# A state-space convolution mixed with an MLP by a gate: the taps' factors, powers and products laid out with each channel's samples side by side

## The chip, the cores and the metric

The kernel runs on one core of one Trainium2 chip. The metric is the device time of one execution in microseconds (us), the median of several runs. The engines are named as in the profile: PE is TensorE (PEld its weight loads), DVE is VectorE, ACT is ScalarE, POOL is GpSimd, SP the queue of SyncE, which issues most of the DMAs.

## What is computed

There are L = 2048 positions, D = 512 channels and NS = 128 states per channel. Branch a is a convolution along the positions, with taps made from the states; branch b is an MLP with 1792 hidden columns; a gate g per position mixes the two.

```python
g = sigmoid((x * gate_w).sum(-1, keepdims=True))
# a: taps K of each channel, then a causal convolution and a skip
P = exp((dt * (A_re + 1j * A_im))[:, :, None] * l)      # l = 0 .. 2047
K = einsum("dn,dnl,dn->dl", C, P, dt * B).real
y = irfft(rfft(pad(K)) * rfft(pad(u)))[:L] + u * Dskip
# b
h = gelu(x @ w1 + b1)
return g * y + (1 - g) * (h @ w2 + b2)
```

The change lies in the making of K.

## The kernel before

**Two parts.** `front` holds the MLP, the first stage of the transforms of the signal and of the taps, and the making of the taps. `conv` loads the transformed signal and taps back from HBM, multiplies them, transforms back and mixes. In the profile `front` fills some 0 to 402 us and `conv` the rest.

**How `front` is ordered.** Every piece of work in `front` is a task of a planner (`Plan`): an engine, a fixed cost, what it reads and writes, and a due time from the list `DUES`. `pl.run()` plays the tasks through once, on the host and with the fixed costs, and issues them in that order. On the chip each engine then works off its own instructions strictly in that order; an instruction whose input is late holds up all those behind it on its engine. The MLP (`hidden`, L985 to L1012; `output`, L1028 to L1060), the signal's first stage (`first_stage`, L489) and the taps are interleaved in this way. The MLP's matmuls are split into high and low halves: ScalarE makes the gelu (L1002) and the high half `hh` (L1005), VectorE the low half `hl` (L1012), TensorE multiplies both.

**The taps.** A tap of channel d at position l = 64 p + q is a sum over the 128 states of a factor for p times a factor for q, both complex. The 512 channels come in four units of 128 (`prepare`, `coefficients`), a unit in four chunks of CW = 32 channels: 16 chunks, each with the same steps, the states on the 128 partitions:

- `phases` (L695, L703), VectorE: 33 phases per channel as 32-bit integers, by doubling, in `ph`, shape [33, 32 channels].
- `waves` (L711 to L713), ScalarE: absolute value, sine and cosine of these 33 x 32 phases, into `tt` (two planes). There is one `tt`; the next chunk's waves wait for the rotation that reads it.
- `begin` (L721), ScalarE: a copy of four starting factors per channel into `xc`.
- `powers` (L594 to L597, through `cmul`), VectorE: three complex doublings, from 4 to 32 factors per channel in `xc`, with scratch `xt_`, `xv_`.
- `magnitudes` (L740 on GpSimd, L752 and L750 on VectorE): 64 magnitudes per channel in `e = y[:, 1]`, by doubling from both ends.
- `rotate` (L763, L770, L774), VectorE: magnitudes times cosine and sine, the real and the imaginary plane of `y`.
- `contract` (L788), TensorE: for each channel a product over the states of its 32 factors (`x`, the weights) with its 64 samples (`y`, the moving operand), in two steps for the real and imaginary plane. Four channels run side by side in four column tiles of 32 columns. They go into the PSUM tile `pk`; VectorE adds the skip term in one column (L804), ScalarE copies the result to `s1` (L807).

After every second chunk `first_stage` (L489) transforms two such results, ScalarE copies them to `sk` (L815), and after every fourth the unit is stored to HBM in eight DMAs (L830). `conv` begins with loads of these (`tk`, L1197).

**Layout before.** In `xc`, `xt_`, `xv_`, `tt` and `y` the channel is the innermost index: the 32 channels of a factor or sample lie side by side, and one channel's samples lie 32 words apart. `pk` is [64 samples, 8 channels]: one channel's samples lie 8 words apart. So L788 reads both of its operands, and writes its result, with a step:

```python
pks[q][32 * j : 32 * j + 32, :, gg],
x[:, r, :, ch],
y[:, r, :, ch],
```

while the operations of VectorE and ScalarE run over neighbouring words, the factors that are the same for all samples being repeated along an outer index.

Of the kernel before, what the change touches and what calls it, by code (L numbers as in the profile page):

```python
# [349 lines left out]
def gated_mix(  # L350
# [52 lines left out]
    def front(pool, psum, keep, attic, loft, den, pr):  # L403
# [28 lines left out]
        pks = tiles(N_PK, [P, 64, 8], "pk", space=psum)  # L432
# [3 lines left out]
        y = pool.tile([P, 2, 64, CW], F32, name="y")  # L436
        xc = [den[:, k : k + 4].rearrange("p k d -> p (k d)").rearrange("p (a b c) -> p a b c", a=2, c=CW) for k in (0, 4)]
        xt_, xv_ = (loft[:, k * 1024 : k * 1024 + 1024].rearrange("p (a b c) -> p a b c", a=2, c=CW) for k in range(2))
        tt = loft[:, 2048:4160].rearrange("p (a b c) -> p a b c", a=2, c=CW)
# [148 lines left out]
        def cmul(due, dst, a, br, bi, n, t, v, ka, kb, kd, kt, kv):  # L588

            w = a.shape[-1]  # L590
            br = br.unsqueeze(1).unsqueeze(1).to_broadcast([P, 2, n, w])
            bi = bi.unsqueeze(1).unsqueeze(1).to_broadcast([P, 2, n, w])
# [116 lines left out]
        def waves(t):  # L709
            def sines():  # L710
                nc.scalar.activation(tt[:, 0], ph, AF.Abs)  # L711
                nc.scalar.activation(tt[:, 1], ph, AF.Sin, scale=TWO_PI / TURN)
                nc.scalar.activation(tt[:, 0], tt[:, 0], AF.Sin, bias=half_pi, scale=-TWO_PI / TURN)  # L713

            act(3.14, sines, t + D_KA, ["ph"], ["tt"], "sin")

        def begin(c, k, t):
# [3 lines left out]
                0.31, lambda: nc.scalar.copy(xc[k][:, :, 0:4], x4[:, :, :, cs]), t + D_KA,  # L721
# [15 lines left out]
        def magnitudes(u, c, t):  # L737

            cs = slice(c * CW, (c + 1) * CW)
            pl.add("POOL", 0.1, lambda: nc.gpsimd.memset(e[:, 63], 1.0), t, [], ["y1"])  # L740

            def both(lo, step, n):

                a = e[:, lo : lo + n].copy()
                return bass.AP(a.tensor, a.offset, [a.ap[0], [step * CW, 2], *a.ap[1:]])

            def double(k):
                n = 1 << k
                an = ea[u % 2][:, k, cs].unsqueeze(1).unsqueeze(1).to_broadcast([P, 2, n, CW])
                nc.vector.tensor_mul(both(n, 64 - 3 * n, n), both(0, 64 - n, n), an)  # L750

            vec(CW, lambda: nc.vector.tensor_copy(e[:, 0], ea[u % 2][:, 5, cs]), t, [("ea", u % 2)], ["y1"])  # L752
# [3 lines left out]
        def rotate(t):  # L756

            v = nc.vector
            cc = tt[:, 0, 0:32]
# [714 lines left out]
```

## Time and profile before

| | |
|---|---|
| runs | 507.99, 508.39, 508.75 us; median 508.39 |
| span of the profiled execution | 505.5 us, so some 2.9 us of the median lie around it |
| TensorE busy | 495.2 us (98%) |
| VectorE busy | 429.2 us (85%) |
| ScalarE busy | 365.0 us (72%) |
| mean granted TensorE clock | 0.996 |

How to read it: a group's row gives line, engine, operation, output and inputs, partitions by elements, type and count, then busy time, the mean of one in ns, and the idle time of its engine just before it with what ended it. A row of a timeline gives start and length in us, engine, line, and, in brackets, idle time before it. A row of a table of stretches gives the stretch, its length, the busy time and count of PE, PEld, DVE, ACT and POOL, the granted clock, the DMA share and GB/s. Matmuls overlap, so the busy time of TensorE holds some latency, and the mean of one is longer than the distance between two starts.

### The profile page before, as it was taken

The page shows a single profiled execution, that of the slowest core. Times are in us where ns is not written, and L with a number is a line of the kernel's source. Part 1 is how long each engine was busy: PE and PEld are TensorE (multiplying, and loading weights), DVE is VectorE, ACT ScalarE, POOL GpSimd, SP SyncE. Part 2 cuts the span into 40 slices and gives each one's busy share as a digit, 9 for nine tenths or more (in the row PEclk, how much of TensorE's full clock was granted, in tenths as well). Part 3 has the DMA queues.
Part 4 walks back from the last instruction along what each step waited for, and adds up shares of the span by engine and source line. Part 5 has one row for each costly group of instructions (what it writes and reads, how often), then busy time and mean ns, then how long its engine had stood idle before and what let it go on. Part 6 is the DMA issues. An engine that isn't in the chain of part 4 may idle for free.

```text
span 505.5 us, 12181 instructions
## 1 busy us (share of the span) xinstructions
PE 495.2 (98%) x4802; PEld 379.0 (75%) x4802; DVE 429.2 (85%) x817; ACT 365.0 (72%) x632; POOL 38.3 (8%) x78
## 2 busy tenths in 40 slices
PE   8999999999999999999999999999999999999994
PEld 7898888898989889888988888998989522222551
DVE  4977999999999999999999999999940197877455
ACT  6999997899997789997767998636834465565310
POOL 2000000000000000001010020110100100231000
PEclk9999999999999999999999999999999999999998
DMA  8978686531858622855987244950477999989897
GB/s 286 350 280 278 188 243 213 161 126 43 280 138 246 200 73 72 254 168 116 232 217 241 75 64 128 186 100 3 154 219 169 259 389 389 338 305 391 294 344 299
DMA packets 81569, 107.56 MB, mean 213 GB/s; under 512 B 39284, under 2 KB 43784, under 8 KB 80968
## 3 DMA queue, kind: packets, MB, share of 16 engines
q1 hardware_dynamic: 74792, 82.80, 51.8%
q0 software_dynamic: 6016, 20.70, 15.4%
q10 hardware_dynamic: 704, 3.28, 1.8%
q8 instruction: 38, 0.62, 0.5%
q14 instruction: 19, 0.16, 0.1%
HBM read 61.14 MB, written 45.62 MB: 211 GB/s over the span
## 4 chain that ended last, share of the span: by engine, by line
PE 93%; DMA 2%; SPq 1%; DVE 1%; issue 1%; ACT 0%; POOL 0%; DVEq 0%; POOLq 0%
PE pk L788 12%; PE ph L985 10%; PE acc L1028 10%; PE ph L987 10%; PE ph L986 10%; PE acc L1029 9%; PE acc L1031 9%; PE p2k L1218 5%; PE p2u L1218 5%; PE pa L1257 3%; PE ph L489 3%; PE pb L1373 2%; DMA tk<-tk_d 1%; SPq L830 1%; DMA tk_d<-sk 1%; PE acc L1101 1%
## 5 line engine op out<-in xcount | busy, mean ns | idle before, releaser
L985 PE MATMUL ph<-xh,wh 128*128 128x256 f32 x448 | 127.5, 285 | 0.0
L987 PE MATMUL ph<-xh,wl 128*128 128x256 f32 x448 | 126.8, 283 | 0.0
L986 PE MATMUL ph<-xlo,wh 128*128 128x256 f32 x448 | 126.7, 283 | 0.0
L985 PEld LDWEIGHTS ph<-xh,wh 128*128 128x128 f32 x448 | 85.2, 190 | 6.9 <-issue 4.0
L986 PEld LDWEIGHTS ph<-xlo,wh 128*128 128x128 f32 x448 | 85.1, 190 | 2.1
L987 PEld LDWEIGHTS ph<-xh,wl 128*128 128x128 f32 x448 | 85.2, 190 | 0.0
L1028 PE MATMUL acc<-wh,hh 128*128 128x512 f32 x208 | 84.3, 405 | 0.0
L1029 PE MATMUL acc<-wl,hh 128*128 128x512 f32 x208 | 81.7, 393 | 0.0
L1031 PE MATMUL acc<-wh,hl 128*128 128x512 f32 x208 | 81.4, 391 | 0.0
L1002 ACT ACTIVATE ph<-ph,b1t 128x256 f32<-128x256 f32 x112 | 50.5, 451 | 25.0 <-PE ph L987 23.2
L788 PE MATMUL pk<-y,den 128*32 128x64 f32 x2048 | 61.4, 290 | 0.0
L788 PEld LDWEIGHTS pk<-y,den 128*32 128x32 f32 x2048 | 57.2, 136 | 2.6 <-issue 0.7
L1012 DVE TENSOR_TENSOR hl<-ph,hh 128x512 fp32r<-128x512 f32 (+1 forms) x62 | 38.2, 618 | 18.3 <-ACT hh L1005 10.8
L1028 PEld LDWEIGHTS acc<-wh,hh 128*128 128x128 f32 x208 | 39.1, 188 | 19.4 <-issue 8.8
L750 DVE TENSOR_TENSOR y<-y,ea 128x64 f32<-128x64 f32 (+4 forms) x80 | 45.3, 566 | 0.8 <-POOL y L740 0.3
L1031 PEld LDWEIGHTS acc<-wh,hl 128*128 128x128 f32 x208 | 39.1, 188 | 8.8
L1029 PEld LDWEIGHTS acc<-wl,hh 128*128 128x128 f32 x208 | 39.1, 188 | 6.1
L1226 ACT COPY k<-p2k 128x512 f32<-128x512 f32 x32 | 18.6, 586 | 27.2 <-issue 11.3
L594 DVE TENSOR_TENSOR loft<-den,zz 128x256 f32<-128x256 f32 (+2 forms) x48 | 37.2, 774 | 0.2
L595 DVE TENSOR_TENSOR loft<-den,zz 128x256 f32<-128x256 f32 (+2 forms) x48 | 37.2, 775 | 0.1
L763 DVE TENSOR_TENSOR y<-y,loft 128x2048 f32<-128x2048 f32 x16 | 36.6, 2286 | 0.4 <-ACT loft L713 0.2
L1005 ACT CAST hh<-ph 128x512 fp32r<-128x512 f32 (+1 forms) x62 | 33.0, 533 | 4.3 <-PE acc L1029 2.4
(197 smaller groups left out, 873.3 us busy)
## 6 DMA issues: line engine op xcount, KB each, us to landing
tk_d<-sk SPq DMA_DIRECT2D x32, 256.0 KB, 5.3
t_d<-sa SPq DMA_DIRECT2D x32, 256.0 KB, 5.1
tu_d<-attic SPq DMA_DIRECT2D x40, 128.0 KB, 3.5
attic<-in_xt_dram SPq DMA_DIRECT2D x16, 256.0 KB, 4.3
attic<-in_xs_dram SPq DMA_DIRECT2D x16, 256.0 KB, 5.0
xl_d<-xlo SPq DMA_DIRECT2D x8, 512.0 KB, 5.9
xh_d<-xh SPq DMA_DIRECT2D x8, 512.0 KB, 3.9
out_dram<-io SPq DMA_DIRECT2D x16, 256.0 KB, 3.1
```

The costliest lines, as they stand in the source:

```text
L594: vec(2 * m, lambda: vv.tensor_mul(t, a, br), due, [ka, *kb], [kt])
L750: nc.vector.tensor_mul(both(n, 64 - 3 * n, n), both(0, 64 - n, n), an)
L788: nc.tensor.matmul(pks[q][32 * j : 32 * j + 32, :, gg], x[:, r, :, ch], y[:, r, :, ch], start=(r == 0), stop=(r == 1), skip_group_check=True,)
L985: nc.tensor.matmul(p, h, xh[xk][:, d], start=(d == 0), stop=False)
L986: nc.tensor.matmul(p, h, xlo[xk][:, d], start=False, stop=False)
L987: nc.tensor.matmul(p, lo, xh[xk][:, d], start=False, stop=(d == 3))
L1002: nc.scalar.activation(phs[q][:, n], phs[q][:, n], AF.Gelu_apprx_tanh, bias=b1t[:, f : f + 1])
L1012: nc.vector.tensor_sub(lo, phs[q][:, 0:nf], hi.bitcast(F32))
L1028: nc.tensor.matmul(a, h, wh[1][w], start=start, stop=False, skip_group_check=seeded)
L1029: nc.tensor.matmul(a, h, wl[1][w], start=False, stop=False, skip_group_check=seeded)
L1031: nc.tensor.matmul(a, l, wh[1][w], start=False, stop=stop, skip_group_check=seeded)
L1218: nc.tensor.matmul(out[64 * i : 64 * i + 64], w, x, start=True, stop=True)
```

## The change

The innermost index becomes the sample: `xc`, `xt_`, `xv_`, `tt` and `y` are laid out with each channel's factors or samples side by side, `pk` as [8 channels, 64 samples]. So L788 reads and writes neighbouring words. The phases `ph` keep their old layout; ScalarE reads them turned (`turned`) in two of its three wave operations, turns the four starting factors in `begin`, and turns the result as it copies it out of PSUM. VectorE's operations keep their counts and elements, with the loops turned: factors that are the same for all samples are now repeated along the innermost index (step 0). The rows of `tt` are 33 words long. `DUES`, the planner's costs and the tasks stay as they are.

```diff
-        pks = tiles(N_PK, [P, 64, 8], "pk", space=psum)
+        pks = tiles(N_PK, [P, 8, 64], "pk", space=psum)
...
-        y = pool.tile([P, 2, 64, CW], F32, name="y")
-        xc = [den[:, k : k + 4].rearrange("p k d -> p (k d)").rearrange("p (a b c) -> p a b c", a=2, c=CW) for k in (0, 4)]
-        xt_, xv_ = (loft[:, k * 1024 : k * 1024 + 1024].rearrange("p (a b c) -> p a b c", a=2, c=CW) for k in range(2))
-        tt = loft[:, 2048:4160].rearrange("p (a b c) -> p a b c", a=2, c=CW)
+        y = pool.tile([P, 2, CW, 64], F32, name="y")
+        xc = [den[:, k : k + 4].rearrange("p k d -> p (k d)").rearrange("p (a c b) -> p a c b", a=2, c=CW) for k in (0, 4)]
+        xt_, xv_ = (loft[:, k * 1024 : k * 1024 + 1024].rearrange("p (a c b) -> p a c b", a=2, c=CW) for k in range(2))
+        tt = loft[:, 2048:4160].rearrange("p (a c b) -> p a c b", a=2, c=CW)
...
-        def cmul(due, dst, a, br, bi, n, t, v, ka, kb, kd, kt, kv):
-
-            w = a.shape[-1]
-            br = br.unsqueeze(1).unsqueeze(1).to_broadcast([P, 2, n, w])
-            bi = bi.unsqueeze(1).unsqueeze(1).to_broadcast([P, 2, n, w])
+        def cmul(due, dst, a, br, bi, n, t, v, ka, kb, kd, kt, kv, inner=False):
+
+            w = CW if inner else a.shape[-1]
+            shape, at = ([P, 2, w, n], 3) if inner else ([P, 2, n, w], 1)
+            br = br.unsqueeze(1).unsqueeze(at).to_broadcast(shape)
+            bi = bi.unsqueeze(1).unsqueeze(at).to_broadcast(shape)
...
-                nc.scalar.activation(tt[:, 0], ph, AF.Abs)
-                nc.scalar.activation(tt[:, 1], ph, AF.Sin, scale=TWO_PI / TURN)
+                turned = ph.rearrange("p b c -> p c b")
+                nc.scalar.activation(tt[:, 0], turned, AF.Abs)
+                nc.scalar.activation(tt[:, 1], turned, AF.Sin, scale=TWO_PI / TURN)
                 nc.scalar.activation(tt[:, 0], tt[:, 0], AF.Sin, bias=half_pi, scale=-TWO_PI / TURN)
...
-                0.31, lambda: nc.scalar.copy(xc[k][:, :, 0:4], x4[:, :, :, cs]), t + D_KA,
+                0.31, lambda: nc.scalar.copy(xc[k][:, :, :, 0:4], x4[:, :, :, cs].rearrange("p a b c -> p a c b")), t + D_KA,
...
-                    t, x[:, :, n : 2 * n], x[:, :, 0:n], zz[:, 0, i, cs], zz[:, 1, i, cs], n,
-                    xt_[:, :, 0:n], xv_[:, :, 0:n], ("xc", k), ["zz"], ("xc", k), "xt", "xv",
+                    t, x[:, :, :, n : 2 * n], x[:, :, :, 0:n], zz[:, 0, i, cs], zz[:, 1, i, cs], n,
+                    xt_[:, :, :, 0:n], xv_[:, :, :, 0:n], ("xc", k), ["zz"], ("xc", k), "xt", "xv", True,
...
-            pl.add("POOL", 0.1, lambda: nc.gpsimd.memset(e[:, 63], 1.0), t, [], ["y1"])
+            pl.add("POOL", 0.1, lambda: nc.gpsimd.memset(e[:, :, 63], 1.0), t, [], ["y1"])
...
-                a = e[:, lo : lo + n].copy()
-                return bass.AP(a.tensor, a.offset, [a.ap[0], [step * CW, 2], *a.ap[1:]])
+                a = e[:, :, lo : lo + n].copy()
+                return bass.AP(a.tensor, a.offset, [a.ap[0], [step, 2], *a.ap[1:]])
...
-                an = ea[u % 2][:, k, cs].unsqueeze(1).unsqueeze(1).to_broadcast([P, 2, n, CW])
+                an = ea[u % 2][:, k, cs].unsqueeze(1).unsqueeze(3).to_broadcast([P, 2, CW, n])
...
-            vec(CW, lambda: nc.vector.tensor_copy(e[:, 0], ea[u % 2][:, 5, cs]), t, [("ea", u % 2)], ["y1"])
+            vec(CW, lambda: nc.vector.tensor_copy(e[:, :, 0], ea[u % 2][:, 5, cs]), t, [("ea", u % 2)], ["y1"])
...
-            cc = tt[:, 0, 0:32]
-            cc = bass.AP(cc.tensor, cc.offset, [cc.ap[0], [CW, 2], *cc.ap[1:]])
+            cc = tt[:, 0, :, 0:32]
+            cc = bass.AP(cc.tensor, cc.offset, [cc.ap[0], [1, 2], *cc.ap[1:]])
...
-                v.scalar_tensor_tensor(e[:, 0:32], e[:, 0:32], -1.0, tt[:, 1, 0:32], ALU.mult, ALU.mult)
+                v.scalar_tensor_tensor(e[:, :, 0:32], e[:, :, 0:32], -1.0, tt[:, 1, :, 0:32], ALU.mult, ALU.mult)
...
-            vec(32 * CW, lambda: v.tensor_mul(e[:, 32:64], e[:, 32:64], tt[:, 1, 1:33]), t, ["tt"], ["y1"])
+            vec(32 * CW, lambda: v.tensor_mul(e[:, :, 32:64], e[:, :, 32:64], tt[:, 1, :, 1:33]), t, ["tt"], ["y1"])
...
-                                pks[q][32 * j : 32 * j + 32, :, gg],
-                                x[:, r, :, ch],
-                                y[:, r, :, ch],
+                                pks[q][32 * j : 32 * j + 32, gg],
+                                x[:, r, ch],
+                                y[:, r, ch],
...
-            at0 = pks[q][:, 63]
+            at0 = pks[q][:, :, 63]
...
-            act(0.48, lambda: nc.scalar.copy(xs, pks[q].rearrange("p s g -> p (s g)")), t + D_S1, [("pk", q)], [key])
+            act(0.48, lambda: nc.scalar.copy(xs.rearrange("p (s g) -> p s g", g=8), pks[q].rearrange("p g s -> p s g")), t + D_S1, [("pk", q)], [key])
```

More of the change, by code (lines that the diff above doesn't have):

```diff
@@ L758, in rotate @@
             v = nc.vector
-            cc = tt[:, 0, 0:32]
-            cc = bass.AP(cc.tensor, cc.offset, [cc.ap[0], [CW, 2], *cc.ap[1:]])
+            cc = tt[:, 0, :, 0:32]
+            cc = bass.AP(cc.tensor, cc.offset, [cc.ap[0], [1, 2], *cc.ap[1:]])
             def real():
                 v.tensor_mul(
-                    y[:, 0].rearrange("p (a b) c -> p a b c", a=2),
-                    e.rearrange("p (a b) c -> p a b c", a=2),
+                    y[:, 0].rearrange("p c (a b) -> p a c b", a=2),
+                    e.rearrange("p c (a b) -> p a c b", a=2),
                     cc,
```

## The prediction

> **What bounds the kernel now.** I read the page first, then the busy time by stage, the waits, the groups of instructions by form, and at the end the timelines of three stretches and of the tail. The median of the three runs is 508.39 us; the span of the profiled execution is 505.5 us, so 2.9 us lie around it. All terms below are changes of this span, put on the median at the end. Some 0.2% (1 us) is what a measurement here can tell from no change.
>
> ```profile
> span 505.5 us, 12181 instructions
> ## 1 busy us (share of the span) xinstructions
> PE 495.2 (98%) x4802; PEld 379.0 (75%) x4802; DVE 429.2 (85%) x817; ACT 365.0 (72%) x632; POOL 38.3 (8%) x78
> ```
>
> This page says that TensorE is the bound. The busy time by stage (columns: stretch and its length, then PE, PEld, DVE, ACT, POOL) says more:
>
> ```profile
> 50.00:372.00 322.00, 321.97 (x3724) 279.32 (x3723) 314.42 (x599) 265.92 (x445) 22.30 (x45) 1.00 0.58 159
> 372.00:402.40 30.40, 29.36 (x300) 23.88 (x298) 4.49 (x8) 12.60 (x26) 1.71 (x2) 1.00 0.79 189
> 402.40:505.50 103.10, 96.14 (x484) 32.85 (x484) 72.35 (x117) 42.79 (x80) 10.04 (x16) 0.98 0.94 345
> ```
>
> While the taps are made (50 to 372 us) TensorE has no idle time, but VectorE has 314.4 of 322 us too: 7.6 us are all that it can give. ScalarE idles 56 us. The last tap, made by VectorE, releases the stores that the last stage (402 us on) must load. So TensorE work saved in this stretch is worth only what VectorE's chain allows. The waits of the same stretch (total, times, longest), of VectorE and then of ScalarE:
>
> ```profile
> DVE pk L804 <- PE pk L788: 2.5, 6, 0.6
> DVE hl L1012 <- ACT hh L1005: 1.2, 4, 0.4
> ```
>
> ```profile
> ACT ph L1002 <- PE ph L987: 13.1, 9, 2.5
> ACT io L1053 <- PE acc L1031: 10.2, 9, 4.0
> ```
>
> VectorE waits for the contraction (L788) 2.5 us in all; ScalarE's longest waits are for TensorE.
>
> **The contraction on TensorE.** Its rows now (matmul and weight load), beside the loads of 64 and of 128 neighbouring columns and the last stage's fp32 matmuls:
>
> ```profile
> L788 PE MATMUL pk<-y,den 128*32 128x64 f32 x2048 | 61.4, 290 | 0.0
> L788 PEld LDWEIGHTS pk<-y,den 128*32 128x32 f32 x2048 | 57.2, 136 | 2.6 <-issue 0.7
> ```
>
> ```profile
> L1373 PEld LDWEIGHTS pb<-t,g1t 128*64 128x64 f32 x52 | 3.7, 137 | 7.0 <-issue 4.9 <-DVE loft L1386 1.4 <-DVE attic L1386 0.3
> ...
> L1308 PEld LDWEIGHTS acc<-wh,xh 128*128 128x128 f32 x8 | 1.5, 187 | 1.9 <-issue 1.6
> ```
>
> ```profile
> 411.64 1.03 PE L1218 MATMUL p2k<-tk,cc 128*64 128x512 f32 x4
> 412.50 1.03 PE L1218 MATMUL p2k<-tk,f 128*64 128x512 f32 x4
> ```
>
> 61.4 us over 16 chunks are 3.84 us per contraction: 128 instructions in 32 rounds of four column tiles, 0.12 us a round, 1.87 ns for each of 64 strided columns. The contiguous L1218 starts four instructions, two rounds of two tiles, in 412.50 - 411.64 = 0.86 us: 0.43 us for 512 columns, 0.84 ns each. The loads agree: 64 more neighbouring columns cost 187 - 137 = 50 ns (0.78 ns each), so 32 should take 137 - 25 = 112 ns; the strided ones take 136, as if each column counted twice. I take a strided element at twice the price of a neighbour, for TensorE. With everything side by side a round is 64 x 0.84 = 54 ns if the load stays hidden, 54 + 25 = 79 ns if it doesn't; a contraction 32 x 54 ns plus some 0.2 us of tail, 1.9 to 2.7 us, taken as 2.0. That is 1.8 us less, 29 us over sixteen, and nearly all of it becomes idle time of TensorE, since VectorE still sets when y is ready.
>
> **What ScalarE takes over.** The phases are now read with a step of 32 words (L711, L712), the results out of PSUM with a step of 64 (L807):
>
> ```profile
> L712 ACT ACTIVATE loft<-phase 128x1056 f32<-128x1056 int32 x16 | 17.5, 1094 | 0.2
> L711 ACT ACTIVATE loft<-phase 128x1056 f32<-128x1056 int32 x16 | 17.5, 1093 | 0.0
> ...
> L807 ACT COPY s<-pk 128x512 f32<-128x512 f32 x16 | 9.4, 587 | 4.2 <-DVE pk L804 4.1
> ```
>
> 1093 - 587 = 506 ns for 544 more elements: 0.93 ns each. No row shows ScalarE reading single strided elements. One bound is no cost; the other is twice the price, as the weight load shows for TensorE: 0.98 us on each of L711 and L712, 0.48 us on L807, 2.4 us per chunk. I take the upper, because the nearest strided rows pay it. The Trainium skill, Vector Engine (DVE) Microarchitecture Reference, section 5.2 "Measured stream behaviour on trn2", says that a VectorE port keeps its full rate only on runs of two or more neighbouring 4-byte words, at 1.05 ns an element against some 1.7 for single hops and 2.5 in one case of a small step. L788 agrees with the first; by 2.5 ns on ScalarE's two phase reads too, a chunk would cost 3.3 us there, the stalls below would double, and the forecast would end near 518 us.
>
> Over 50 to 372 us the 2.4 us x 14 chunks = 34 us fit into ScalarE's 56 us. They don't fit where it has no idle time just ahead of the rotation (L763), which waits for its sines. Three stretches that end at such a rotation (columns as above), and the instructions at their ends:
>
> ```profile
> 47.10:51.90 4.80, 4.80 (x32) 4.27 (x31) 4.76 (x17) 4.75 (x6) 0.41 (x1) 1.00 1.03 341
> 190.10:225.40 35.30, 35.30 (x445) 30.18 (x444) 34.29 (x67) 34.72 (x64) 2.36 (x6) 1.00 0.51 156
> 277.30:304.70 27.40, 27.40 (x393) 24.27 (x392) 26.37 (x55) 26.62 (x47) 3.11 (x6) 1.00 0.36 85
> ```
>
> ```profile
> 50.54 1.17 ACT L713 ACTIVATE loft<-loft,half_pi 128x1056 f32<-128x1056 f32 x1
> ```
>
> ```profile
> 51.88 2.28 DVE L763 TENSOR_TENSOR y<-y,loft 128x2048 f32<-128x2048 f32 x1
> ```
>
> ```profile
> 225.40 2.29 DVE L763 TENSOR_TENSOR y<-y,loft 128x2048 f32<-128x2048 f32 x1 [0.18 <-ACT loft L713]
> ```
>
> ```profile
> 303.23 1.16 ACT L713 ACTIVATE loft<-loft,half_pi 128x1056 f32<-128x1056 f32 x1
> ```
>
> ```profile
> 304.69 2.29 DVE L763 TENSOR_TENSOR y<-y,loft 128x2048 f32<-128x2048 f32 x1
> ```
>
> ```profile
> 275.89 0.93 ACT L1002 ACTIVATE ph<-ph,b1t 128x256 f32<-128x256 f32 x2 [2.48 <-PE ph L987]
> ```
>
> These are the rotations of chunks 0, 8 and 12, the first of a unit, which wait for one set of waves (chunk 0) or come behind two sets and two L807. Chunk 0: 1.96 us more, 0.17 of slack (51.88 less 51.71): 1.8 us. Chunk 8: 4.9 us more, 35.30 - 34.72 = 0.6 idle: 4.3 us, less what ScalarE is early when the stretch begins. Chunk 12: 4.9 - 0.8 idle - 0.3 slack = 3.8 us, less up to 2.5 us that ScalarE waited for TensorE just before, at 275.89, and which a faster contraction can give back. I take 1.8 + 3.0 + 1.5 = 6.3 us, between 1.8 and 9.9. Behind the waiting rotation VectorE's whole queue stands (the low halves L1012, the next powers), and TensorE's contraction waits for y. For low halves that come late in between I add 1 us (0 to 3). The turned copy of the four starting factors (L721, 256 elements) has no place in the two long stretches and I cost it at nothing; its cover is ScalarE's 56 us of idle time.
>
> **VectorE.** Instruction counts and elements stay.
>
> ```profile
> L763 DVE TENSOR_TENSOR y<-y,loft 128x2048 f32<-128x2048 f32 x16 | 36.6, 2286 | 0.4 <-ACT loft L713 0.2
> ...
> L750 DVE TENSOR_TENSOR y<-y,ea 128x64 f32<-128x64 f32 x16 | 3.5, 220 | 0.5 <-POOL y L740 0.3
> ```
>
> (2286 - 220) / (2048 - 64) = 1.04 ns an element. Runs of 4 to 32 neighbours should keep that. Single strided elements are left in the smallest doubling (64) and in the copy ahead of it (32); rows of tt, 33 words apart, begin off an even word in half of the cases, and I allow two lone elements for each of those 64 rows: 224 elements at some 0.7 ns extra (1.87 less 1.04, rounded down), 0.16 us a chunk, 2.5 us over sixteen (0 to 5). GpSimd's memset of 32 elements (L740), now lone ones, holds the first doubling up for 0.3 us in all; I add nothing for it. The broadcast factors now repeat along the innermost step; no row shows that, and I cost it at nothing here (rival below). The 2.5 us of waits at L804 go, because the contraction ends earlier: -2.5 us.
>
> **The tail.** From the last y to the last stage:
>
> ```profile
> 369.29 1.22 DVE L774 TENSOR_TENSOR y<-y,loft 128x1024 f32<-128x1024 f32 x1
> ```
>
> ```profile
> 372.74 3.83 PE L788 MATMUL pk<-y,den 128*32 128x64 f32 x128
> ```
>
> ```profile
> 376.85 0.59 ACT L807 COPY s<-pk 128x512 f32<-128x512 f32 x1 [2.45 <-DVE pk L804]
> ```
>
> ```profile
> 378.13 0.64 PE L489 MATMUL ph<-s,c1t 32*64 32x512 f32 x2
> ```
>
> ```profile
> 402.36 4.24 PE L1218 MATMUL p2k<-tk,pr 128*64 128x512 f32 x16 [1.04 <-DMA tk<-tk_d]
> ```
>
> y is ready at 370.5, but TensorE gets there at 372.74: 2.2 us go when it has time to spare. The contraction is 1.8 us shorter, L489 no longer comes 0.7 us after its input (377.44), L807 costs 0.5 us more: -4.2 us. Stores and loads up to 402.36 move along, and so does TensorE's dense work behind the last contraction; the last stage is untouched.
>
> **Sum:** 6.3 + 1 + 2.5 - 2.5 - 4.2 = +3.1 us, 511.5 us. With the bounds of the terms this case reaches from 506 to 518 us.
>
> **Rivals.**
> First, faster: ScalarE reads the turned phases at its old rate, so the 6.3 + 1 us and the 0.5 us fall away. 2.5 - 2.5 - 4.7 = -4.7 us: 503.7 us. For it: a gather by one engine is not a matmul's weight load, and ScalarE's rows show no strided read. Against: both strided rows of TensorE pay double. It decides from about half of my price on, where the three stalls (some 3 us) no longer outweigh the tail.
> Second, the change doesn't do what it says: the round of 0.12 us is not the step but four tiles drawing four streams out of the same partitions (no row has four tiles on neighbours, and two tiles at 0.84 ns a column draw nearly as much as four at 1.87). Then TensorE has no time to spare, the stalls are at their upper 9.9 us, nothing is won at L804, only the 2.2 us in the tail close up behind a later y: 9.9 + 1 + 2.5 - 2.2 + 0.5 = +11.7, 520 us. Against it stands the weight load of 136 ns. The Trainium skill, TensorEngine Tiling (Array Packing), section "Instruction Overhead", gives each matmul about 60 cycles however small it is; if that added up over four tiles, a round would stay near its present length. It doesn't add up in this trace, where the eight tiled matmuls of a first stage start within 0.04 us:
>
> ```profile
> 69.47 0.59 PE L489 MATMUL ph<-attic,c1t 32*64 32x512 f32 x1
> ```
>
> ```profile
> 69.51 0.59 PE L489 MATMUL pu<-ux,c1t 32*64 32x512 f32 x1
> ```
>
> Third, slower by far: a factor repeated along the innermost step is read like lone elements. Powers and doublings hold 5568 such elements a chunk (3584 + 1984); at 0.7 ns that is 3.9 us, 62 us over sixteen on an engine with 7.6 us to give: about 565 us.
>
> **How the numbers follow.** Forecast case 0.57, ScalarE at full rate 0.26, contraction unchanged 0.10, repeated factors dear 0.05, anything else 0.02. The range takes in the first two with their bounds, 502.5 to 519 us (the forecast's own: 506 to 518), and leaves out some 0.17. Faster: 0.25 of the second case and 0.06 of the first, 0.31. Within 0.2%: 0.08 of the first and 0.01 of the second, 0.09. Slower: the rest, 0.60.
>
> **What would show it.** In the profile after, L788 should fall from 61.4 to some 32 us and its weight load to about 112 ns; L711 and L712 should rise to 2.0 us, L807 to 1.1; L713, L770 and the powers (L594, L595) should stay within 3%; the waits should show VectorE's L763 on ScalarE's L713 with some 6 us and L804 on L788 with almost none; TensorE should idle some 25 us before the last stage. L711 at 1.1 us, or a sum of waits at L763 under 2 us, would make the forecast wrong towards faster; L788 still at 3.8 us, or L594 well above 1.2 us for 1024 elements, towards slower.

## The result and the profile after

The changed kernel takes 528.22 us (median; 508.19 us for the kernel before on the same chip): 1.039 times as long, 95% interval 1.036 to 1.042. The profiled execution spans 525.9 us, 20.4 us more than the 505.5 us before. The median counts all four executions, one of which ran at a granted clock of 0.66 and took 657 us; the other three have a median of 527.6 us, and the ratio is theirs.

In the changed kernel the lines stand one or two lower than before: the contraction is L790 (before L788), the three instructions of the waves L713 to L715 (L711 to L713), the copy of the starting factors L723 (L721), the rotation L765, L772, L776 (L763, L770, L774), the copy out of PSUM L809 (L807), high and low halves L1007 and L1014 (L1005, L1012), the first add of the phases L704 (L703).

First the page, its busy time by engine:

```profile
PE 483.0 (92%) x4802; PEld 354.1 (67%) x4802; DVE 431.1 (82%) x817; ACT 402.2 (76%) x632; POOL 38.7 (7%) x78
```

TensorE is busy for 12 us less, VectorE for 2 us more, ScalarE for 37 us more, and no engine is busy throughout any more: TensorE has gone from 98% to 92%, VectorE from 85% to 82%. A span that grows while its busiest engine is busy for less has grown by waits. Where they lie shows in the same stretch as before (columns: stretch and its length, PE, PEld, DVE, ACT, POOL):

```profile
50.00:372.00 322.00, 291.92 (x3481) 239.26 (x3480) 294.90 (x570) 286.43 (x427) 19.69 (x40) 0.98 0.54 148
```

In these 322 us TensorE now idles for 30 us and VectorE, which had 314.4 us of work before, for 27 us. The groups of instructions by form (busy time, mean ns of one, then idle time before them and its releaser):

```profile
L714 ACT ACTIVATE loft<-phase 128x1056 f32<-128x1056 int32 x16 | 35.1, 2193 | 0.2
L713 ACT ACTIVATE loft<-phase 128x1056 f32<-128x1056 int32 x16 | 35.1, 2191 | 1.0 <-DVE phase L696 1.0
...
L790 PE MATMUL pk<-y,den 128*32 128x64 f32 x2048 | 32.8, 220 | 4.0 <-DVE y L776 2.1 <-ACT attic L507 1.7
...
L790 PEld LDWEIGHTS pk<-y,den 128*32 128x32 f32 x2048 | 29.6, 110 | 7.3 <-issue 3.2 <-ACT attic L507 2.2
...
L723 ACT COPY den<-x 128x256 f32<-128x256 f32 x16 | 10.2, 654 | 3.8 <-DVE x L598 3.4 <-PE pk L790 0.4
...
L809 ACT COPY s<-pk 128x512 f32<-128x512 f32 x16 | 9.3, 584 | 7.0 <-DVE pk L806 7.0
...
L752 DVE TENSOR_TENSOR y<-y,ea 128x64 f32<-128x64 f32 x16 | 4.4, 272 | 0.3
...
L754 DVE COPY y<-ea 128x32 f32<-128x32 f32 x16 | 3.2, 199 | 0.0
```

The contraction has fallen from 61.4 to 32.8 us. The two turned readings have doubled, from 1093 to 2192 ns: 35 us in all. The turned reading of PSUM (L809) costs nothing. VectorE's waits, from 45 us on to the last rotation (line waiting, its releaser: us in total, times, longest):

```profile
DVE hl L1014 <- ACT hh L1007: 9.8, 11, 2.4
DVE phase L704 <- ACT loft L714: 7.2, 8, 1.5
DVE y L765 <- ACT loft L715: 4.1, 3, 2.3
DVE xlo L891 <- ACT xh L889: 1.9, 1, 1.9
DVE loft L596 <- ACT den L723: 1.1, 1, 1.1
DVE wl L891 <- ACT wh L889: 0.9, 3, 0.5
DVE loft L649 <- ACT loft L637: 0.6, 1, 0.6
```

All of them are for ScalarE, 25.6 us together. The same view of before, from 45 us to its last rotation, held 4.7 us: these two lines and 0.7 us in three smaller ones (L750, L889, L763).

```profile
DVE pk L804 <- PE pk L788: 2.5, 6, 0.6
DVE hl L1012 <- ACT hh L1005: 1.5, 5, 0.4
```

25.6 - 4.7 = 20.9 us of waits and the 1.9 us of work that VectorE has more (431.1 - 429.2) make 22.8 us. The last tap (end of the last L776) comes at 391.68 + 1.22 = 392.9 us, 22.4 us later than the 370.5 us before, as the first line of the timeline shows:

```profile
391.68 1.22 DVE L776 TENSOR_TENSOR y<-y,loft 128x1024 f32<-128x1024 f32 x1
...
393.57 1.99 PE L790 MATMUL pk<-y,den 128*32 128x64 f32 x128
...
396.06 0.59 ACT L809 COPY s<-pk 128x512 f32<-128x512 f32 x1 [0.84 <-DVE pk L806]
...
397.62 0.65 PE L489 MATMUL ph<-s,c1t 32*64 32x512 f32 x2
...
400.51 0.61 ACT L817 COPY sk<-ph 128x512 f32<-128x512 f32 x1
```

In the chain of waits, the first load of the last stage releases its first matmul, 423.39 - 392.9 = 30.5 us after the last tap; before it was 402.36 - 370.5 = 31.9 us:

```profile
416.16 7.19 DMA tk<-tk_d
423.39 0.64 PE p2k L1220
```

22.4 us later, a tail 1.4 us shorter and a last stage 0.6 us shorter (525.9 - 423.39 = 102.5 against 103.1): 20.4 us, the whole difference of the spans. The loss lies between 45 and 392 us, in VectorE's waits for ScalarE.

### The profile page after: what moved, and what is told of

Same layout as the page of the kernel before. It is cut to its first block, busy times and chain, and to the rows that moved or that the text cites. A ratio compares the mean times of both kernels' runs of the same rounds, so it can differ in the third digit from the quotient of the medians.

```text
span 525.9 us, 12185 instructions
## 1 busy us (share of the span) xinstructions
PE 483.0 (92%) x4802; PEld 354.1 (67%) x4802; DVE 431.1 (82%) x817; ACT 402.2 (76%) x632; POOL 38.7 (7%) x78
## 4 chain that ended last, share of the span: by engine, by line
PE 38%; ACT 33%; DVE 16%; issue 6%; DMA 4%; SPq 1%; POOL 0%; DVEq 0%; ACTq 0%; POOLq 0%
PE p2k L1220 5%; PE p2u L1220 5%; ACT loft L713 4%; ACT loft L714 4%; PE ph L987 4%; ACT ph L1004 4%; PE ph L988 4%; PE ph L989 4%; PE pa L1259 3%; PE acc L1033 3%; PE acc L1030 3%; ACT L1004 2%; PE acc L1031 2%; DVE y L752 2%; ACT hh L1007 2%
## 5 line engine op out<-in xcount | busy, mean ns | idle before, releaser
L987 PE MATMUL ph<-xh,wh 128*128 128x256 f32 x448 | 128.7, 287 | 10.7 <-ACT sk L817 4.3
L1030 PE MATMUL acc<-wh,hh 128*128 128x512 f32 x208 | 86.3, 415 | 7.8 <-ACT hh L1007 3.6
L1033 PE MATMUL acc<-wh,hl 128*128 128x512 f32 x208 | 83.9, 403 | 4.3 <-DVE hl L1014 4.1
L1031 PE MATMUL acc<-wl,hh 128*128 128x512 f32 x208 | 83.2, 400 | 0.0
L1004 ACT ACTIVATE ph<-ph,b1t 128x256 f32<-128x256 f32 x112 | 50.6, 452 | 22.2 <-PE ph L989 20.4
L1014 DVE TENSOR_TENSOR hl<-ph,hh 128x512 fp32r<-128x512 f32 (+1 forms) x62 | 38.4, 620 | 26.1 <-ACT hh L1007 17.5
L765 DVE TENSOR_TENSOR y<-y,loft 128x2048 f32<-128x2048 f32 x16 | 36.6, 2290 | 4.3 <-ACT loft L715 4.1
L596 DVE TENSOR_TENSOR loft<-den,zz 128x256 f32<-128x256 f32 (+2 forms) x48 | 37.3, 777 | 1.2 <-ACT den L723 1.1
L595 DVE TENSOR_TENSOR loft<-den,zz 128x256 f32<-128x256 f32 (+2 forms) x48 | 37.3, 778 | 0.2
L790 PE MATMUL pk<-y,den 128*32 128x64 f32 x2048 | 32.8, 220 | 4.0 <-DVE y L776 2.1
L713 ACT ACTIVATE loft<-phase 128x1056 f32<-128x1056 int32 x16 | 35.1, 2191 | 1.0 <-DVE phase L696 1.0
L1007 ACT CAST hh<-ph 128x512 fp32r<-128x512 f32 (+1 forms) x62 | 32.9, 531 | 3.7 <-PE acc L1031 1.8
```

What stands on the lines that cost most here:

```text
L713: nc.scalar.activation(tt[:, 0], turned, AF.Abs)
L987: nc.tensor.matmul(p, h, xh[xk][:, d], start=(d == 0), stop=False)
L1004: nc.scalar.activation(phs[q][:, n], phs[q][:, n], AF.Gelu_apprx_tanh, bias=b1t[:, f : f + 1])
L1007: nc.scalar.copy(hi, phs[q][:, 0:nf])
L1014: nc.vector.tensor_sub(lo, phs[q][:, 0:nf], hi.bitcast(F32))
L1030: nc.tensor.matmul(a, h, wh[1][w], start=start, stop=False, skip_group_check=seeded)
```

## The experiments

Theory A: the loss is ScalarE's doubled reading of the phases, and nothing else in the change costs anything that matters. Rival B: it is something else of the change, the broadcast factors, VectorE's lone elements or the new order of TensorE's and VectorE's work. Later runs ask by which doors the time gets from ScalarE to VectorE, which of the three strides on TensorE was the dear one, and whether the turning can be had more cheaply.

**1. The changed kernel with flat readings.** ScalarE reads neighbours again, so that a sine belongs to another sample; all else of the change stays.

```
-                turned = ph.rearrange("p b c -> p c b")
+                turned = ph.rearrange("p b c -> p (b c)").rearrange("p (c b) -> p c b", c=CW)
```

> The changed kernel, but ScalarE reads the phases in the order in which they lie, so the sines belong to other samples (the phases of channel and sample are mixed up; everything else is computed as before). Theory A (the whole loss is ScalarE's turned phase reads, 2.2 us instead of 1.1 us each, which reach VectorE as late high halves, late sines and a phase tile that is still being read): both reads at 1.1 us, VectorE's waits back under 6 us, 502 to 506 us. Rival B (the shorter contraction upsets the order that was planned for the old length, and TensorE's clock falls in its idle gaps): only part comes back, 513 us or more.

500.97 us, ratio 0.989 (0.986 to 0.992). The busy time of the stretch and VectorE's only wait up to its last rotation:

```profile
50.00:372.00 322.00, 306.12 (x3878) 257.03 (x3878) 315.09 (x603) 271.12 (x449) 22.78 (x45) 1.00 0.59 162
```

```profile
DVE hl L1014 <- ACT hh L1007: 2.4, 3, 1.8
```

VectorE is back at 315 of 322 us, its waits for ScalarE are gone but for 2.4 us, and TensorE has 16 us to spare. The time is 1 us under the 502 to 506 us that A expected. Beside the kernel before on the same chip (507.2 us) the change without the turning is worth 6 us, and the turning costs 528.2 - 501.0 = 27.2 us.

**2. The kernel before with turned readings.** The other half alone (ScalarE writes the phases' values straight on, in the old tile; the sines belong to other samples):

```
-                nc.scalar.activation(tt[:, 0], ph, AF.Abs)
-                nc.scalar.activation(tt[:, 1], ph, AF.Sin, scale=TWO_PI / TURN)
+                turned = ph.rearrange("p b c -> p c b")
+                t0, t1 = (tt[:, k].rearrange("p b c -> p (b c)").rearrange("p (c b) -> p c b", c=CW) for k in range(2))
+                nc.scalar.activation(t0, turned, AF.Abs)
+                nc.scalar.activation(t1, turned, AF.Sin, scale=TWO_PI / TURN)
```

> The kernel before, with nothing changed but the two phase reads, which ScalarE now does with the step of 32 words (the sines belong to other samples). Theory A: ScalarE's 35 us more cost what they cost in the changed kernel, and TensorE with its long contraction has no time to spare: 525 to 535 us. Rival B: the order is the old one and TensorE stays busy, so little is lost: under 516 us.

529.9 us, ratio 1.045 (1.043 to 1.047). The groups by form; in this kernel the readings are L713 and L714:

```profile
L790 PE MATMUL pk<-y,den 128*32 128x64 f32 x2048 | 61.8, 290 | 3.2 <-ACT attic L507 1.8 <-DVE y L776 1.4
...
L713 ACT ACTIVATE loft<-phase 128x1056 f32<-128x1056 int32 x16 | 35.9, 2243 | 1.2 <-DVE phase L695 1.2
L714 ACT ACTIVATE loft<-phase 128x1056 f32<-128x1056 int32 x16 | 35.5, 2217 | 0.2
```

The old contraction, the old layout everywhere else, and still the whole loss: B has fallen. VectorE waits at the same places as in the changed kernel, 8.8 us at the low halves, 7.9 us at the next phases, 4.1 us at the rotation.

**3. Turning on the way out.** The phases are read straight, and ScalarE writes `tt` with a step of 33 words instead:

```
-                nc.scalar.activation(tt[:, 0], turned, AF.Abs)
-                nc.scalar.activation(tt[:, 1], turned, AF.Sin, scale=TWO_PI / TURN)
+                t0, t1 = (tt[:, k].rearrange("p c b -> p b c") for k in range(2))
+                nc.scalar.activation(t0, ph, AF.Abs)
+                nc.scalar.activation(t1, ph, AF.Sin, scale=TWO_PI / TURN)
```

> The changed kernel, but ScalarE reads the phases as they lie and turns them when it writes (step of 33 words on the write). If a strided write costs like a strided read, both operations stay at 2.2 us and the time at 522 to 532 us; if writes are free of it, they take 1.1 us and theory A expects 502 to 506 us, rival B 513 us or more.

526.8 us, ratio 1.039 (1.037 to 1.041):

```profile
L714 ACT ACTIVATE loft<-phase 128x1056 f32<-128x1056 int32 x16 | 35.7, 2233 | 0.2
```

2.23 us written with a step (2.245 on the other one, L713), 2.19 us read with one: between these two tiles in SBUF ScalarE has no cheap side on which to turn.

**4. The planner told the measured costs.** Waves 5.35 us instead of 3.14, the starting copy 0.56 instead of 0.31, half a contraction 0.98 instead of 1.83:

```
-            act(3.14, sines, t + D_KA, ["ph"], ["tt"], "sin")
+            act(5.35, sines, t + D_KA, ["ph"], ["tt"], "sin")
```

> The changed kernel, with three costs in the host's planner set to what was measured (waves 5.35 instead of 3.14, the starting factors' copy 0.56 instead of 0.31, half a contraction 0.98 instead of 1.83), so that the order on each engine changes and no instruction does. Theory A: ScalarE's work is still 35 us more; a better order wins back some of the waits, 510 to 526 us. Rival B: the order was the cause, 508 us or less.

577.95 us, ratio 1.139 (1.132 to 1.145): neither expectation held. Another order of the work comes out, and its longest waits of VectorE are

```profile
DVE hl L1014 <- ACT hh L1007: 27.9, 13, 4.8
DVE pk L806 <- PE pk L790: 12.6, 10, 6.3
```

With new costs and the old due times the high halves come still later; that the due times, which were set for the old costs, are the reason was not tested. This says nothing for or against A. It shows that the order can cost more (50 us here, part of it at a lower granted clock, 0.938 against 0.986) than the thing changed, and that correcting the costs alone is no remedy.

**5. Half the dose.** Only the Abs is read turned:

```
-                nc.scalar.activation(tt[:, 1], turned, AF.Sin, scale=TWO_PI / TURN)
+                flat = ph.rearrange("p b c -> p (b c)").rearrange("p (c b) -> p c b", c=CW)
+                nc.scalar.activation(tt[:, 1], flat, AF.Sin, scale=TWO_PI / TURN)
```

> The changed kernel, but of ScalarE's two readings of the phases only the first (Abs) is turned; the second (Sin) reads the phases flat, so its sines belong to other samples. ScalarE then pays 1.1 us a chunk instead of 2.2. Theory A (ScalarE's lateness reaches VectorE by several doors, and each microsecond of it in the taps' stretch costs nearly one): half of the 27 us between flat reads (501.0) and the changed kernel (528.2), 512 to 517 us, with VectorE's waits for hh and for the phases' readers some 10 us. Rival D (ScalarE has room for a first microsecond per chunk, and only what goes beyond it is paid): under 507 us.

512.1 us, ratio 1.010 (1.0075 to 1.012). The first 17.6 us on ScalarE (16 x 1.10) cost 512.1 - 501.0 = 11.1 us, the second 17.6 us cost 528.2 - 512.1 = 16.1 us. The runs were not all made on one chip; with each set against the kernel before on its own chip, and with 527.6 us for the changed kernel, the halves are 10.7 and 15.0 us. D has fallen: there was no room for a first microsecond. ScalarE's 51 idle microseconds of the flat kernel (322 - 271) absorbed some 40% of the first half and 10 to 15% of the second.

**6. The phases turned once.** ScalarE's time stays at 5.5 us a chunk, but the tile `ph` comes free after the first 2.2 us:

```
-                nc.scalar.activation(tt[:, 0], turned, AF.Abs)
-                nc.scalar.activation(tt[:, 1], turned, AF.Sin, scale=TWO_PI / TURN)
+                nc.scalar.copy(tt[:, 1], turned)
+                nc.scalar.activation(tt[:, 0], tt[:, 1], AF.Abs)
+                nc.scalar.activation(tt[:, 1], tt[:, 1], AF.Sin, scale=TWO_PI / TURN)
```

> The changed kernel, with one turned reading of the phases instead of two: a copy into the place of the sines (2.19 us), then Abs and Sin from there over neighbours (1.09 us each) and the last Sin as before (1.16 us). ScalarE's time per chunk stays the same, 5.5 us, but the phases' tile is free after the first 2.19 us instead of after 4.38. Theory A with two doors: VectorE's waits at the next phases (L704, 7.2 us in the changed kernel) go and the time falls by most of that, to 520 to 523 us. Rival G (ScalarE's time is what counts; a wait taken away at one door comes back at the next, the high halves hh): within 2 us of the changed kernel, 526 to 530 us.

532.4 us, ratio 1.049 (1.045 to 1.052) to the kernel before, so 4 us longer than the changed kernel. VectorE's longest waits (lines one lower):

```profile
DVE hl L1015 <- ACT hh L1008: 15.1, 12, 2.9
DVE y L766 <- ACT loft L716: 6.4, 3, 2.3
```

No wait at the next phases is left in the view, and the other doors have taken them over: 15.1 us at the low halves instead of 9.8, 6.4 at the rotation instead of 4.1. The run is not a clean one, though. Its copy writes into the plane of the sines, which the last rotation of the chunk before still reads, and so ScalarE begins later:

```profile
L713 ACT CAST loft<-phase 128x1056 f32<-128x1056 int32 x16 | 34.9, 2178 | 4.9 <-DVE y L777 3.7 <-DVE phase L696 1.2
```

These 3.7 us of waiting do not exist in the changed kernel and may be the 4 us that it is longer. Even without them the time would, by this estimate, be some 528 us, where G had it (526 to 530), and not the 520 to 523 of two doors. So the time that ScalarE needs in its queue counts for more here than the tile that it holds.

**7 and 8. The phases made by GpSimd, in turned order.** GpSimd adds them up as [channel][sample], so ScalarE reads neighbours; the other engines keep their order:

```
-        ph = pool.tile([P, 33, CW], I32, name="phase")
+        ph = pool.tile([P, CW, 33], I32, name="phase")
...
-                nc.vector.tensor_tensor(
-                    ph[:, n + 1 : 2 * n + 1],
-                    ph[:, 1 : n + 1],
-                    ph[:, n].unsqueeze(1).to_broadcast([P, n, CW]),
+                nc.gpsimd.tensor_tensor(
+                    ph[:, :, n + 1 : 2 * n + 1],
+                    ph[:, :, 1 : n + 1],
+                    ph[:, :, n].unsqueeze(2).to_broadcast([P, CW, n]),
```

> The changed kernel, but the phases are added up by GpSimd instead of VectorE, and in the turned order from the start (tile of 32 channels by 33 samples), so ScalarE reads neighbours; nothing else moves in any engine's order. It takes 1.97 us a chunk (31 us in all) from VectorE and gives ScalarE its 1.09 us reads back. No row of the runs so far shows GpSimd adding. If its six adds of a chunk stay under some 6 us together, theory A expects less than the 501.0 us of flat reads: TensorE was idle for 16 us of the stretch from 50 to 372 us there, and with VectorE 28 us freer most of that goes: 485 to 497 us. Rival: GpSimd's adds are so long (over 10 us a chunk) or disturb VectorE so much that the sines come late, and the rotations wait for them: 505 us or more.

507.7 us, ratio 1.001 (0.9996 to 1.002): the turning is free for ScalarE (its readings take 1.09 us again), but the time is that of the kernel before, not the 485 to 497 us that A expected; the rival had 505 us or more. One group of VectorE, in the kernel with flat readings and then in this one:

```profile
L752 DVE TENSOR_TENSOR y<-y,ea 128x128 f32<-128x128 f32 x16 | 4.6, 285 | 0.1
```

```profile
L752 DVE TENSOR_TENSOR y<-y,ea 128x128 f32<-128x128 f32 x16 | 7.1, 445 | 0.1
```

While GpSimd adds (80 us more busy time on its page), VectorE's own instructions take longer: this one by 160 ns, all groups together by 22 us, of the 31.5 us that the phases had taken. Rows of one engine overlap in part; on the pages, which count no moment twice, VectorE is busy for 430.1 us against 428.9 with flat readings, so nothing at all was freed. The rival's other half, sines that come late at the rotations, did not happen: no wait of VectorE there is left. The Trainium skill, GPSIMD Engine Reference, section "Specifications", says that GpSimd shares its SBUF interfaces with VectorE and contends with instructions that have two SBUF inputs; this row's doublings multiply two such inputs, and the trace agrees.

The same with the kernel before (phases by GpSimd in their old order):

> The kernel before, with the phases added up by GpSimd in their old order (33 samples by 32 channels); nothing else is touched. VectorE has 31 us less to do, but TensorE had no idle time from 50 to 372 us, so theory A (the change is worth what VectorE and ScalarE leave of it) expects little: 503 to 508 us, and the distance to the changed kernel with GpSimd's phases is what the turned products are worth once nobody pays for the turning, 10 to 20 us. Rival (VectorE, not TensorE, was the bound of the kernel before): 495 us or less.

511.7 us, ratio 1.009 (1.006 to 1.0115): a loss of 4 us where A expected a small gain. TensorE is busy for 319.68 of 322 us in the stretch and was the bound, as expected; but it idles there for 2.3 us, which it did not before, and its own busy time is 1.9 us longer (497.1 against 495.2), and its last rotation starts 4.6 us later (373.9 against 369.29). VectorE had no time freed here either: its page has it busy for 433.7 us, against 429.2 before. Between 511.7 and 507.7 us the turned products are worth 4 us here, not the 10 to 20 us that were expected.

**9. One GpSimd copy that turns.** VectorE adds the phases as before, GpSimd copies 1056 words, turned, to where the sines will stand:

```
-                turned = ph.rearrange("p b c -> p c b")
+                turned = tt[:, 1].bitcast(I32)
+                nc.gpsimd.tensor_copy(turned, ph.rearrange("p b c -> p c b"))
```

> The changed kernel, with the phases left to VectorE in their old order and turned once per chunk by one GpSimd copy of 1056 words into the place where the sines will stand; both of ScalarE's readings then take neighbours from there. Nothing else moves in any engine's order. GpSimd's largest add of the last runs took 1.19 us for 512 elements, so 1056 should take 1.5 to 2.5 us, between the last add and the sines. Theory A: ScalarE is at its old 1.09 us a reading again, VectorE keeps its 31 us of phases and loses, by the 22 us that 81 us of GpSimd's adds cost it before, some 7 to 11 us to 16 copies: 503 to 512 us. Rival E (VectorE's instructions are lengthened by what GpSimd's adds do, not by a plain copy): 499 to 503 us. Rival F (the extra hand-over makes the sines late at every rotation): over 515 us.

540.1 us, ratio 1.064 (1.059 to 1.068). GpSimd's copy, from the groups, and ScalarE's longest wait:

```profile
L713 POOL COPY loft<-phase 128x1056 int32<-128x1056 int32 x16 | 43.5, 2717 | 131.1 <-DVE y L777 60.9 <-DVE phase L696 49.3 <-ACT st L507 21.0
```

```profile
ACT loft L714 <- POOL loft L713: 37.9, 14, 4.8
```

F had the number, but not the reason. The copy can begin only when the last rotation has left `tt` or the last add is done (its idle time says so), takes 2.7 us, and ScalarE stands in its queue for it 37.9 us, about as long as the turned readings cost it. But the rotations hardly wait for the sines. What has grown is VectorE's own work (its page, one group, its wait at the rotation):

```profile
PE 488.3 (91%) x4802; PEld 357.1 (66%) x4802; DVE 456.9 (85%) x817; ACT 369.2 (69%) x632; POOL 80.7 (15%) x94
```

```profile
L597 DVE TENSOR_TENSOR den<-loft 128x256 f32<-128x256 f32 x16 | 12.6, 785 | 0.2
```

```profile
DVE y L766 <- ACT loft L716: 0.2, 1, 0.2
```

VectorE is busy for 456.9 us, against 428.9 with flat readings, and this product takes 785 ns instead of 419; one of them, begun while a copy ran, took 1.71 us. The last tap comes 37 us later than with flat readings; from 45 us up to it VectorE is busy for 27 us more and idle for 11 us more. So most of this loss is VectorE beside a working GpSimd, and rival E, that a plain copy lengthens nothing, has fallen.

**10 to 12. Which stride was the dear one?** Each is the kernel with flat readings with one of the contraction's three operands stepped again; the moving operand's edit is

```
-                                y[:, r, ch],
+                                y[:, r].rearrange("p c s -> p (c s)").rearrange("p (s c) -> p s c", c=CW)[:, :, ch],
```

> The kernel with flat phase reads, with the contraction's moving operand alone (y, 64 columns) taken again with a step of 32 words; products mix other samples and channels. If the moving stream sets the contraction's length, the round of four column tiles goes back from 62 to some 113 to 120 ns (L790 from 32.8 to about 61 us) and the weight load stays at 110 ns. If the load of the weights sets it, L790 stays near 33 us.

```profile
L790 PE MATMUL pk<-y,den 128*32 128x64 f32 x2048 | 60.1, 289 | 0.0
L790 PEld LDWEIGHTS pk<-y,den 128*32 128x32 f32 x2048 | 55.8, 126 | 2.6 <-ACT attic L507 0.4 <-issue 0.4
```

506.8 us (one execution each from here on). The weight load did not stay at 110 ns, as expected, though its own operand lies side by side: 126 ns.

> The kernel with flat phase reads, with the contraction's weights alone (x, 32 columns) taken again with a step of 32 words; products mix other samples and channels. If the moving stream sets the contraction's length, L790 stays near 33 us and the weight load alone goes from 110 to about 136 ns. If the load sets it, L790 goes back to some 61 us.

```profile
L790 PE MATMUL pk<-y,den 128*32 128x64 f32 x2048 | 35.0, 224 | 1.2 <-DVE y L776 1.1
L790 PEld LDWEIGHTS pk<-y,den 128*32 128x32 f32 x2048 | 32.4, 141 | 4.2 <-issue 1.8 <-ACT attic L507 0.4
```

501.3 us.

> The kernel with flat phase reads, with the contraction's output alone written into PSUM again with a step of 8 words; the results land at other places. If writing is limited as reading is, L790 goes back to some 61 us; if a strided PSUM write costs TensorE nothing, it stays near 33 us, as ScalarE's strided PSUM read cost nothing (584 against 587 ns).

```profile
L790 PE MATMUL pk<-y,den 128*32 128x64 f32 x2048 | 32.8, 220 | 1.6 <-DVE y L776 1.4
```

501.2 us. The moving operand alone makes the contraction dear (60.1 of the old 61.4 us). Stepped weights cost their load 31 ns and the contraction 2 us, a stepped output nothing. So, as far as the contraction goes, of the change's turned tiles only `y` was worth turning, and `y` is the one that needs turned sines. That VectorE could turn on its own side, by reading `tt` with a step in the rotation, was not tried.

No run in which every sine stays with its sample beats the kernel before; the one with GpSimd's phases draws level.

## Why the prediction was wrong

The direction was forecast (slower, chance 0.60), the size was not: 511.5 us, range 502.5 to 519, against 528.2. (Taken all at once, the bounds of its terms give 503.5 to 519.6 us, not the stated 506 to 518; 528.2 lies outside both.) By its steps:

- **The contraction**: 2.0 us a chunk, 32 us in all, weight load 112 ns; measured 2.05 us (32.8 / 16), 32.8 us, 110 ns. Right, and so was the reason, neighbours instead of steps, though hardly for the weights: experiments 10 to 12 put it on the moving operand. The second rival (four streams) has fallen: the round of four tiles went from 0.12 to 0.064 us, 32.8 / 512. So the overhead weighed there (the Trainium skill, TensorEngine Tiling (Array Packing), section "Instruction Overhead", some 60 cycles for each matmul however small) does not hold the round of four column tiles at its old length, as the prediction had argued.
- **The turned readings**: 0.98 us each, from TensorE's rows; measured 1.10 us. Right. Taking the rate from another engine's row was the nearest that the trace had, and experiment 1 shows that what the first rival supposed, ScalarE at full rate, would have made it 501.0 us (forecast for that rival: 503.7).
- **The turned PSUM copy**: 0.48 us; measured nothing (584 ns against 587). Wrong, and small.
- **The starting copy**, costed at nothing: 654 ns instead of 407, 4 us more on ScalarE. The kernel with flat readings carries them too and is faster than the one before, so no run shows that they cost anything by themselves.
- **The stalls of VectorE behind ScalarE: the step that failed.** It said that the 34 us of added work "fit into ScalarE's 56 us" and would be felt only at the rotations of chunks 0, 8 and 12, 6.3 us (1.8 to 9.9), with 1 us (0 to 3) for low halves that come late. The rotations did wait at these three chunks and at no other, 0.88, 2.34 and 0.88 us. Two of these waits on VectorE:

```profile
52.61 0.19 DVE L704 CUSTOM_DVE_ANT_0 phase<-phase,ti 128x64 uint16<-128x64 uint16 x1 [1.07 <-ACT loft L714]
53.68 2.29 DVE L765 TENSOR_TENSOR y<-y,loft 128x2048 f32<-128x2048 f32 x1 [0.88 <-ACT loft L715]
...
241.06 2.29 DVE L765 TENSOR_TENSOR y<-y,loft 128x2048 f32<-128x2048 f32 x1 [2.34 <-ACT loft L715]
```

At chunks 0 and 12 VectorE had stood 1.07 us for the same waves just before (L704, the first row), so some 6.2 us were lost there: this term was right. Everywhere else it had allowed 1 us, and 17.7 us came. 8.3 us were low halves waiting for their high halves (9.8 - 1.5). 5.1 us were the next chunk's first phase (7.2 us at L704 less the 2.1 just named), which may not overwrite `ph` until ScalarE's second reading is done; before, L703 had no such wait, and the prediction did not name this door at all. Another 4.3 us were smaller hand-overs (L891, L596, L649). Less the 2.5 us gone at L804 and 0.5 us of small waits before, VectorE waited 20.9 us more in all. Experiment 6 suggests that listing doors one by one would not have helped: the door at L704 closed, and its 7.2 us came out of the others. Experiment 5, run afterwards, gives the price that the sum lacked: some 60% of each added microsecond in the first half of the dose and 85 to 91% in the second, so 27 us for 35 us.
- **Why the 56 us were not room.** ScalarE's idle time before was waiting: for TensorE (13.1 us at L1002, 10.2 at L1053) and others, at places that the fixed order set. Work put behind such a gap starts late whatever its length, and work queued behind the waves (the gelu and the high halves of the MLP) is late with it. This is read from the views; the runs show its price, not each single gap. This timeline of the changed kernel shows one chunk's waves on ScalarE,

```profile
255.83 2.19 ACT L713 ACTIVATE loft<-phase 128x1056 f32<-128x1056 int32 x1
258.03 1.28 ACT L714 ACT_TABLE_LOAD   x1
259.33 2.13 ACT L714 ACTIVATE loft<-phase 128x1056 f32<-128x1056 int32 x1
```

with no gap in it (the line in the middle loads ScalarE's table for the sines), and VectorE's next phase waiting for its end:

```profile
261.49 0.19 DVE L704 CUSTOM_DVE_ANT_0 phase<-phase,ti 128x64 uint16<-128x64 uint16 x1 [1.24 <-ACT loft L714]
```

- **VectorE's lone elements**: 2.5 us; its busy time rose by 1.9 us (429.2 to 431.1), the smallest doubling from 220 to 272 ns, the copy ahead of it from 174 to 199. About right in sum; the rows of `tt`, for which more than half of it was allowed, cost next to nothing (the rotation 2286 to 2290 ns). The broadcast factors were free, as costed (L594, now L595, 1221 ns for 1024 elements before, 1222 after), so the third rival has fallen.
- **L804's waits**, 2.5 us, are gone, as forecast.
- **The tail**: -4.2 us; measured -1.4. From the last tap to the last copy into `sk` it took 401.1 - 392.9 = 8.2 us, against 10.8 before (the first row below), 2.6 us less; L489 still came 1.0 us after its input, because TensorE's dense work lay before it. What lies behind, stores and load, took 1.2 us more, and it is the load: 7.19 us against 5.76 (the second row). Why it took longer stays open.

```profile
380.72 0.62 ACT L815 COPY sk<-ph 128x512 f32<-128x512 f32 x1
...
396.56 5.76 DMA tk<-tk_d
```

So one term of the sum decides. The forecast had 6.3 + 1 - 2.5 = 4.8 us more waits of VectorE; with the measured 20.9 in their place the same sum gives 3.1 - 4.8 + 20.9 = 19.2 us, 527.6 us. The price of a single hop, for which the prediction weighed the Trainium skill, Vector Engine (DVE) Microarchitecture Reference, section 5.2 (1.7 to 2.5 ns on VectorE), came out between those figures on ScalarE: 2192 ns for 1056 elements are 2.1 ns each, the instruction's fixed part included.

## What to carry to other kernels

In a kernel whose engines hand work round in a fixed order, idle time of an engine is not room: before putting work there, ask for each idle piece what it waits for, and charge most of the added time (here some 60 to 90%) unless a run shows otherwise. A layout is paid where it is turned: find the one operand whose step is dear (one run for each operand told it here) and turn only that, on the engine with room, or not at all when the prize, 6 us here, is smaller than the turning. Before moving work to GpSimd, look at what VectorE does beside it: here its busy time did not fall when its adds were taken away. And a wait that is taken away at one tile can come back at the next while the engine behind it stays as late as it was.

## What the runs showed of the hardware

- ScalarE takes twice as long over 1056 single elements a step of 32 words apart, 2192 against 1093 ns, and as long when it writes them with a step of 33 words (2233 and 2245 ns); out of PSUM a step of 64 words cost it nothing (584 against 587 ns for 512).
- TensorE's fp32 matmul, here with 64 moving columns in four column tiles, is slowed by a step in the moving operand (60.1 against 32.8 us), hardly by one in the weights (35.0), and not at all by one in its PSUM output (32.8). The Trainium skill, PSUM — Partial Sum Buffer, section "Specifications (TRN2)", says that any access to PSUM that is not contiguous slows matmuls significantly; the third run shows no such thing for a step of 8 words here, and the measurement decides.
- GpSimd's adds lengthened VectorE's instructions by 22 us over 80 us of adding; its turned copies of 1056 words took 2.7 us each, and over 43.5 us of them VectorE's instructions grew by 29 us. What grew were mostly products and differences of two tiles in SBUF; the low halves, which read one of their two inputs from PSUM, did not (684 ns with flat readings, 683 and 687 in the two runs).
- Where TensorE idled much more, its granted clock was lower too in these runs: in the stretch from 50 to 372 us 1.00 before, 0.98 in the changed kernel (30 us idle) and 0.90 in experiment 4 (55 us idle).
